# Batches 1 and 2 turned through HBM in an FFT convolution with routed experts

## The chip, the cores and the metric

The kernel runs on one core of one Trainium2 chip. The metric is the device time of one execution in microseconds, the median of the runs. Below, TensorE is PE in the rows, VectorE is DVE, ScalarE is ACT, GpSimd is POOL and SyncE is SP; SyncE issues most DMAs, in order, and GpSimd issues the indirect and the accumulating ones.

## The reference

A convolution over the sequence by FFT, then a mixture of 8 experts with a capacity of 768 tokens each:

```python
X = np.fft.rfft(x, axis=1)                       # x: 8 x 3072 x 256
Y = X * (filt_r + 1j * filt_i)[None]
y = np.fft.irfft(Y, n=3072, axis=1)              # rows of the experts: 24576 x 256
logits = x @ w_gate                              # x is now y, flattened
expert_idx = np.argmax(logits, axis=1)           # first 768 tokens of each expert are kept
h = np.maximum(np.einsum('ecd,edf->ecf', disp, w1), 0.0)
y = np.einsum('ecf,efd->ecd', h, w2)
out[i] = gate_w[i] * y[expert_idx[i], pos[i]]    # zero where not kept
```

## The kernel before

Capacity fills up within the first three of eight batches, so only these are convolved; a guarded branch does all eight if that isn't so. For each batch the FFT is split as 3072 = 96 x 32 (N1 = 96, N2 = 32).

**Forward, first stage** (`a`, L257, matmul in L267). The batch's x comes in eight chunks c of four columns t, each 96 partitions x 4 x 256 fp32 (`load_x`, 384 KB). For each t and each half h of the 256 channels, one fp32 matmul has the x piece (96 x 128) as stationary operand and 128 columns of the constant A as moving operand. The result has the channels on the partitions and is copied by ScalarE into ZA[h] (L271).

**Turn** (`t`, L282, transposes in L290). Six steps k transpose ZA in pieces of 64 x 64 on TensorE; ScalarE copies the two banks of a step to Q (L295), which has (frequency part, t) on its 128 partitions, 24 groups p and 256 channels. For batch 0 some copies are VectorE's.

**Middle stage** (`middle`, L354), six groups g with two halves each. `bm` (L303) multiplies Q with the second-stage constants, VectorE makes the products with the filter (L319), GpSimd adds the pairs (L323, L324), `g` (L336) turns them back, ScalarE and VectorE split that into yh and yl (L339, L340), `bi` (L350) runs the inverse second stage, and ScalarE copies the result to V (L352). Between the halves of the groups stand fill steps, a list of lists: one entry after each half from g = 1 on. They hold the routing of the batch before, zero fills of the output (`zero`, 2 MB each), x loads, and in the last middle stage the first expert's weights.

**Inverse, first stage** (`ai`, L396, matmul in L405). VectorE transposes V in four parts (`ti`, L394); 11 steps for half 0 and 8 for half 1 multiply by AI, ScalarE copies to rt (five buffers) and SyncE stores to ybuf (L411).

**Order around the change.** All is written out by hand, engine by engine in program order. For batch b + 1: four chunks of the first stage, inverse half 0 of batch b, the other four chunks interleaved with the routing's counts (`counts`), the small counting matmuls (L493, L494), six turn steps interleaved with `slots`, then inverse half 1 of batch b with the routing's one-hot masks and table matmuls (L548), and the middle stage of b + 1. The last two inverse steps and the rest of the table run in that middle stage (`ahead`, `fill`).

**Weights of expert 0.** `load_part` gives one load of 1 MB to raw (`load_a`, L694) and four cut steps; a cut copies a quarter to wah and its negative to wal on ScalarE (L699, L703), and after every second cut GpSimd issues a DMA that adds the raw weights to wal (L707). `early_row` gathers rows of ybuf on GpSimd (L568). In the last middle stage the four cuts stand in fill entries 0 to 3.

A tile pool named side holds A, the x chunks and ZA, and is closed ahead of the last middle stage; the expert weights take its place.

Of the kernel before, what the change touches and what calls it, by code (L numbers as in the profile page):

```python
# [9 lines left out]
F32 = mybir.dt.float32  # L10
# [78 lines left out]
def fftconv_moe_kernel(ctx, tc, x, x0, fr, fi, fny, wg, w1, w2, ca, cai, cb, co, out, cap):  # L89
# [23 lines left out]
    yall = dram.tile([NB, N1, N2, CH], F32, name="yall")  # L113
    yrows = ybuf.rearrange("b a t c -> (b a t) c")

    def bank():
        return psum.tile([128, 512], F32, name="ps", tag="ps")
# [45 lines left out]
    def run(fs):  # L163
        for f in fs:
            f()

    class Conv:
# [83 lines left out]
        def load_x(self, b, c):  # L251
            t = self.side.tile([N1, 4, D], F32, name="xt", tag="xt")
            src = x[b] if isinstance(b, int) else x[bass.ds(b, 1)].rearrange("o c a t d -> (o c) a t d")
            nc.sync.dma_start(out=t, in_=src[c])
            self.xts[c] = t
# [13 lines left out]
        def a_out(self, ps, c, h):  # L269
            w = 128 if self.resident else QP  # L270
            nc.scalar.copy(self.ZA[h][:, :, c * 4:c * 4 + 4], ps[:, :4 * w].rearrange("p (t q) -> p q t", q=w)[:, :QP, :])  # L271

# [527 lines left out]
    with tc.manual_schedule():  # L800
# [46 lines left out]
        def rows_in(b, cs, more):  # L847
            steps = []
            for c in cs:
                steps += [lambda c=c: cv.a(c, 0), lambda c=c: cv.a(c, 1)]  # L850
                if more:
                    steps.append(lambda c=c: cv.load_x(b, c + 4))
            return steps

        for b in range(NB0 - 1):
            for c in range(4):
                cv.load_x(b + 1, c)
            cv.middle(V, with_zeros(fill, (3, 6)), ahead)
# [5 lines left out]
            run(rows_in(b + 1, range(4), True))  # L864
            run(halves[0])
            interleave(rows_in(b + 1, range(4, 8), False), counts)
            sums()
            interleave([lambda k=k: cv.t(k) for k in range(NP // 4)], slots)
            if b + 2 == NB0:
# [5 lines left out]
                load_a()  # L875
            S = halves[1]
            run([masks[0], masks[1], S[0], S[1], table[0], masks[2], S[2], S[3], table[1], masks[3], S[4], S[5]])
            ahead = S[6:]
            fill = [[table[2]], table[3:]]

# [22 lines left out]
        fill[0].append(cut_a[0])  # L903
        fill[1] += [early_index, cut_a[1]]
        fill += [[cut_a[2], lambda: early_row(0, 0)], [cut_a[3], load_b, lambda: early_row(0, 1)], [lambda: early_row(0, 2)], [last_fill],
# [198 lines left out]
```

## Time and profile before

| | us |
|---|---|
| median of 3 runs | 491.63 |
| lowest, highest | 491.21, 492.63 |
| profiled execution, whole | 493.73 |
| its span | 492.0 |
| TensorE busy | 478.8 |
| ScalarE busy | 270.4 |
| VectorE busy | 243.3 |
| GpSimd busy | 199.4 |

The first 192 us are the three batches, the rest the experts. A row of the timeline has its start from the span's begin, its length, the engine, the line, the operation, tiles and shapes; xN joins N instructions, and brackets give the idle time ahead of it and what ended that. An fp32 matmul is shown as two instructions (two passes). The chain of waits is followed back from the last instruction.

### The profile page before, as it was taken

The page shows a single profiled execution, that of the slowest core. Times are in us where ns is not written, and L with a number is a line of the kernel's source. Part 1 is how long each engine was busy: PE and PEld are TensorE (multiplying, and loading weights), DVE is VectorE, ACT ScalarE, POOL GpSimd, SP SyncE. Part 2 cuts the span into 40 slices and gives each one's busy share as a digit, 9 for nine tenths or more (in the row PEclk, how much of TensorE's full clock was granted, in tenths as well). Part 3 has the DMA queues.
Part 4 walks back from the last instruction along what each step waited for, and adds up shares of the span by engine and source line. Part 5 has one row for each costly group of instructions (what it writes and reads, how often), then busy time and mean ns, then how long its engine had stood idle before and what let it go on. Part 6 is the DMA issues. An engine that isn't in the chain of part 4 may idle for free.

```text
span 492.0 us, 10406 instructions
## 1 busy us (share of the span) xinstructions
PE 478.8 (97%) x4078; PEld 470.9 (96%) x4078; DVE 243.3 (49%) x549; ACT 270.4 (55%) x626; POOL 199.4 (41%) x243
## 2 busy tenths in 40 slices
PE   8999999999999999999999999999999999999994
PEld 8999999999999999999999999999999999899994
DVE  3587755777737878956432343333423423423510
ACT  3555767456657687665362683383482572573411
POOL 3064120444010885518532754454463462563022
PEclk9999999999999999999999999999999999999999
DMA  8997180890645559377458699979979989984001
GB/s 302 340 329 273 33 225 19 213 381 8 162 112 165 113 150 191 90 216 124 115 158 244 143 228 268 365 200 271 367 209 269 362 208 268 351 158 115 0 24 48
DMA packets 60186, 96.16 MB, mean 195 GB/s; under 512 B 4224, under 2 KB 36704, under 8 KB 60000
## 3 DMA queue, kind: packets, MB, share of 16 engines
q1 hardware_dynamic: 43472, 63.55, 40.0%
q0 software_dynamic: 15344, 29.76, 27.9%
q10 hardware_dynamic: 1312, 2.10, 1.3%
q8 instruction: 34, 0.56, 0.5%
q14 instruction: 24, 0.20, 0.1%
HBM read 55.02 MB, written 40.37 MB: 194 GB/s over the span
## 4 chain that ended last, share of the span: by engine, by line
PE 50%; issue 17%; DMA 14%; POOL 10%; DVE 3%; ACT 3%; POOLq 1%; SPq 0%; ACTq 0%; DVEq 0%
DMA y<-ob,idxs 13%; PE ps L608 10%; PE ps L267 8%; PE ps L660 7%; PE ps L405 6%; PE ps L303 5%; PE ps L336 5%; PE ps L350 4%; POOL rows L568 4%; POOL y L666 2%; POOL wal L707 2%; PE ps L429 2%; POOL wbl L707 1%; PE ps L290 1%; DMA V<-x 1%
## 5 line engine op out<-in xcount | busy, mean ns | idle before, releaser
L660 PE MATMUL ps<-wbh,h 128*128 128x256 f32 x768 | 140.8, 283 | 0.0
L591 DVE SCALAR_TENSOR_TENSOR h<-ps,h 128x384 fp32r<-128x384 f32 x128 | 66.7, 552 | 109.8 <-ACT h L589 94.8
L660 PEld LDWEIGHTS ps<-wbh,h 128*128 128x128 f32 x768 | 119.9, 190 | 0.8 <-issue 0.4
L660 PE MATMUL ps<-wbl,h 128*128 128x256 f32 x384 | 108.3, 282 | 0.7 <-issue 0.7
L666 POOL DMA_INDIRECT y<-ob,idxs x48 | 48.6, 1012 | 115.5 <-ACT ob L663 109.0
L608 PE MATMUL ps<-xh,wah 128*128 128x384 f32 x256 | 86.6, 338 | 1.9 <-ACT ob L663 1.8
L608 PE MATMUL ps<-xl,wah 128*128 128x384 f32 x256 | 86.2, 337 | 0.4 <-DVE xl L593 0.4
L608 PE MATMUL ps<-xh,wal 128*128 128x384 f32 x256 | 86.0, 336 | 0.0
L589 ACT ACTIVATE h<-ps 128x384 fp32r<-128x384 f32 x128 | 58.8, 497 | 37.2 <-PE ps L608 29.4
L660 PEld LDWEIGHTS ps<-wbl,h 128*128 128x128 f32 x384 | 72.9, 190 | 0.9 <-issue 0.9
L663 ACT ACTIVATE ob<-ps,gt 128x256 f32<-128x256 f32 x48 | 22.4, 474 | 80.2 <-PE ps L660 38.8
L323 POOL TENSOR_TENSOR t<-t,t 128x256 f32<-128x256 f32 x33 | 24.9, 755 | 68.4 <-DVE t L319 64.0
L608 PEld LDWEIGHTS ps<-xh,wah 128*128 128x128 f32 x256 | 48.1, 188 | 3.1 <-ACT ob L663 2.9
L568 POOL DMA_INDIRECT rows<-ybuf,idxg x42 | 42.8, 1019 | 16.3 <-issue 11.6
L608 PEld LDWEIGHTS ps<-xl,wah 128*128 128x128 f32 x256 | 48.1, 188 | 0.9 <-DVE xl L593 0.9
L608 PEld LDWEIGHTS ps<-xh,wal 128*128 128x128 f32 x256 | 48.1, 188 | 0.0
L336 PE MATMUL ps<-IG,t 128*128 128x136 f32 x288 | 38.2, 281 | 0.8 <-POOL t L324 0.8
L339 ACT CAST yh<-ps 128x408 fp32r<-128x408 f32 x48 | 23.9, 503 | 27.5 <-PE ps L336 26.0
L593 DVE TENSOR_TENSOR xl<-ps,xh 128x384 fp32r<-128x384 f32 x32 | 16.3, 547 | 44.0 <-ACT xh L589 36.1
L336 PEld LDWEIGHTS ps<-IG,t 128*128 128x128 f32 x288 | 35.4, 190 | 1.5 <-POOL t L324 1.4
L303 PE MATMUL ps<-Bc,Q 128*128 128x128 f32 x288 | 35.8, 276 | 0.0
L303 PEld LDWEIGHTS ps<-Bc,Q 128*128 128x128 f32 x288 | 33.8, 192 | 0.1
(135 smaller groups left out, 772.6 us busy)
## 6 DMA issues: line engine op xcount, KB each, us to landing
y<-zt SPq DMA_DIRECT2D x12, 2048.0 KB, 20.5
raw<-w SPq DMA_DIRECT2D x13, 1024.0 KB, 6.2
wbl<-w POOLq DMA_DIRECT2D x16, 512.0 KB
wal<-w POOLq DMA_DIRECT2D x14, 512.0 KB
xt<-x SPq DMA_DIRECT2D x16, 384.0 KB, 5.9
ybuf<-rt SPq DMA_DIRECT2D x20, 162.0 KB, 2.5
ybuf<-rt SPq DMA_DIRECT2D x16, 192.0 KB, 2.9
Q<-x SPq DMA_DIRECT2D x4, 528.0 KB, 8.3
```

The lines of the kernel that those rows point to most:

```text
L267: nc.tensor.matmul(ps[:, i * w:(i + 1) * w], xt[:, i, h * 128:(h + 1) * 128], A[:, i * QP:i * QP + w], start=True, stop=True)
L303: nc.tensor.matmul(ps[:, i * 128:(i + 1) * 128], self.Q[:, p, h * 128:(h + 1) * 128], self.Bc[:, 1 if p == NP - 1 else 0, :], start=True, ...
L323: eng.tensor_tensor(out=t1[:, :, 0, :], in0=t1[:, :, 0, :], in1=t2[:, :, 1, :], op=ALU.subtract)
L336: nc.tensor.matmul(ps[:, i * 136:(i + 1) * 136], self.ysb[(p // 4, h)][:, (p % 4) * 128:(p % 4 + 1) * 128], self.IG[:, h, :], start=True, ...
L339: nc.scalar.copy(fh[:, o], ps[:, :408])
L405: nc.tensor.matmul(ps[:N1, i * w:(i + 1) * w], AI[:, n0 + i, :], V[h][:, :, n0 + i, :], start=True, stop=True)
L568: nc.gpsimd.indirect_dma_start(out=rows[:, t, :], out_offset=None, in_=yrows[:lim, :], in_offset=bass.IndirectOffsetOnAxis(ap=idx[:, j + t ...
L589: nc.scalar.activation(out=hi, in_=ps, func=AF.Relu if relu else AF.Copy)
L591: nc.vector.scalar_tensor_tensor(out=lo, in0=ps, scalar=0.0, in1=hi.bitcast(F32), op0=ALU.max, op1=ALU.subtract)
L608: nc.tensor.matmul(ps[:, :n * 128], w[:, kk, m * 128:(m + 1) * 128], y[:, kk, o], start=k == 0, stop=k == 5)
L660: nc.tensor.matmul(ps[:, :D], y[:, m, o], w[:, m, :], start=m == 0 and j == 0, stop=m == NF - 1 and j == 2)
L666: ins = nc.gpsimd.indirect_dma_start(out=out, out_offset=bass.IndirectOffsetOnAxis(ap=(idxs if ix is None else ix)[:, j:j + 1], axis=0), i ...
```

## The change

Batch 0 stays. For batches 1 and 2 the first stage has the constants A as stationary operand and a whole x row of 256 channels as moving operand (`a_rows`), so that frequencies lie on the partitions. ScalarE copies two banks of a chunk to a slot of ZA[0] (three slots), and SyncE stores it to a new HBM tensor zturn, 96 rows of 4 KB. When all eight chunks are stored, six loads of 512 KB in pieces of 1 KB (`load_Q`) bring it to Q in the order that the transposes made before. Chunks 4 to 6 of x lie in slots of ZA[1].

The x loads of the next batch move into the fill entries 0 to 3 (in batch 2 behind the last three loads of Q), the zero fills from entries 3 and 6 to 5 and 7. The first block of chunks is three, not four; the counts are interleaved with three chunks and the slots with two. The first weight load of expert 0 moves from ahead of inverse half 1 into fill entry 0 of the last middle stage, its four cuts from entries 0 to 3 into 2 and 3, two each.

```diff
         def load_x(self, b, c):
-            t = self.side.tile([N1, 4, D], F32, name="xt", tag="xt")
+            if self.resident and 4 <= c < NCH - 1:
+                t = self.slot(1, c - 4).rearrange("p (t d) -> p t d", d=D)
+            else:
+                t = self.side.tile([N1, 4, D], F32, name="xt", tag="xt")
...
+        def slot(self, h, k):
+            return self.ZA[h].rearrange("p q t -> p (q t)")[:N1, k * 4 * D:(k + 1) * 4 * D]
+
+        def a_rows(self, c):
+
+            xt, A, z = self.xts.pop(c), self.Ac[c], self.slot(0, c % 3)
+            for k in range(2):
+                ps = bank()
+                for i in range(2):
+                    t = 2 * k + i
+                    nc.tensor.matmul(ps[:QP, i * D:(i + 1) * D], A[:, t * QP:(t + 1) * QP], xt[:, t, :], start=True, stop=True)
+                nc.scalar.copy(z[:, k * 2 * D:(k + 1) * 2 * D], ps[:QP, :])
+            nc.sync.dma_start(out=zturn[:, c * 4:c * 4 + 4, :], in_=z.rearrange("p (t d) -> p t d", d=D))
+
+        def load_Q(self, k):
+
+            src = zturn[k * 16:k * 16 + 16].rearrange("(p j) t c -> (j t) p c", p=4)
+            nc.sync.dma_start(out=self.Q[:, k * 4:k * 4 + 4, :], in_=src)
...
-        def rows_in(b, cs, more):
+        def rows_in(b, cs):
             steps = []
             for c in cs:
-                steps += [lambda c=c: cv.a(c, 0), lambda c=c: cv.a(c, 1)]
-                if more:
-                    steps.append(lambda c=c: cv.load_x(b, c + 4))
+                steps.append(lambda c=c: cv.a_rows(c))
+                if c == 0:
+                    steps.append(lambda: cv.load_x(b, NCH - 1))
             return steps
 
+        loads = []
         for b in range(NB0 - 1):
-            for c in range(4):
-                cv.load_x(b + 1, c)
-            cv.middle(V, with_zeros(fill, (3, 6)), ahead)
+            loads += [lambda b=b, c=c: cv.load_x(b + 1, c) for c in range(NCH - 1)]
+            fill = with_zeros(fill, (5, 7))
+            for i, f in enumerate(loads):
+                fill[i // 2].append(f)
+            cv.middle(V, fill, ahead)
...
-            run(rows_in(b + 1, range(4), True))
+            run(rows_in(b + 1, range(3)))
             run(halves[0])
-            interleave(rows_in(b + 1, range(4, 8), False), counts)
+            interleave(rows_in(b + 1, range(3, 6)), counts)
             sums()
-            interleave([lambda k=k: cv.t(k) for k in range(NP // 4)], slots)
+            interleave(rows_in(b + 1, range(6, 8)), slots)
...
-                load_a()
-            S = halves[1]
-            run([masks[0], masks[1], S[0], S[1], table[0], masks[2], S[2], S[3], table[1], masks[3], S[4], S[5]])
+            S, Q = halves[1], [lambda k=k: cv.load_Q(k) for k in range(NG)]
+            run([Q[0], masks[0], masks[1], S[0], S[1], table[0], masks[2], S[2], Q[1], S[3], table[1], masks[3], S[4], Q[2], S[5]])
             ahead = S[6:]
             fill = [[table[2]], table[3:]]
+            loads = Q[3:]
...
-        fill[0].append(cut_a[0])
-        fill[1] += [early_index, cut_a[1]]
-        fill += [[cut_a[2], lambda: early_row(0, 0)], [cut_a[3], load_b, lambda: early_row(0, 1)], [lambda: early_row(0, 2)], [last_fill],
+        fill[0] += [loads[0], load_a]
+        fill[1] += [early_index] + loads[1:]
+        fill += [[cut_a[0], cut_a[1], lambda: early_row(0, 0)], [cut_a[2], cut_a[3], load_b, lambda: early_row(0, 1)],
+                 [lambda: early_row(0, 2)], [last_fill],
                  [cut_b[0]], [cut_b[1]], [cut_b[2]], [cut_b[3], lambda: early_gate(0)]]
```

The lines of the changed kernel are up to 27 later: L287 is the matmul of `a_rows`, L289 its store, L294 the load of Q, L326 and L359 the matmuls that were L303 and L336, L434 the inverse store that was L411, L717, L722 and L730 the weight load, cut and accumulating DMA that were L694, L699 and L707.

SyncE's program before, from the last x loads of batch 2 through its inverse stores into the last middle stage (AI and constants are loaded long before; both is a small constant):

```order
L254 DMA xt<-x 96x1024 x4
L411 DMA ybuf<-rt 96x3x144 x10
L411 DMA ybuf<-rt 96x2x144
L694 DMA raw<-w 128x2x1024
L411 DMA ybuf<-rt 96x4x128 x6
L762 DMA both<-co 128x144
L411 DMA ybuf<-rt 96x4x128 x2
L694 DMA raw<-w 128x8x256
```

SyncE's program with the change, the same place:

```order
L289 DMA zturn<-ZA_97 96x1024 x5
L294 DMA Q<-zturn 128x4x256
L434 DMA ybuf<-rt 96x4x128 x3
L294 DMA Q<-zturn 128x4x256
L434 DMA ybuf<-rt 96x4x128 x2
L294 DMA Q<-zturn 128x4x256
L434 DMA ybuf<-rt 96x4x128
L785 DMA both<-co 128x144
L434 DMA ybuf<-rt 96x4x128 x2
L294 DMA Q<-zturn 128x4x256
L717 DMA raw<-w 128x2x1024
L294 DMA Q<-zturn 128x4x256 x2
```

The first load of Q stands behind the last five stores and ahead of the inverse stores of half 1, and the weight load raw has moved from ahead of these stores to behind them and four loads of Q.

GpSimd's program before, in the last middle stage, from the pairs of group 1 to the second gather (the t tiles are the products; the two instructions of a pair carry one number):

```order
L323 TENSOR_TENSOR t_2212<-t_2212,t_2213 128x8x32
L324 TENSOR_TENSOR t_2212<-t_2212,t_2213 128x8x32
L707 DMA wal<-w 128x1024
L323 TENSOR_TENSOR t_2259<-t_2259,t_2260 128x8x32
L324 TENSOR_TENSOR t_2259<-t_2259,t_2260 128x8x32
L568 DMA rows_2147<-ybuf,idx_72 128x272
L323 TENSOR_TENSOR t_2275<-t_2275,t_2276 128x8x32
L324 TENSOR_TENSOR t_2275<-t_2275,t_2276 128x8x32
L707 DMA wal<-w 128x1024
L568 DMA rows_2147<-ybuf,idx_72 128x272
```

GpSimd's program with the change, the same place:

```order
L346 TENSOR_TENSOR t_1927<-t_1927,t_1928 128x8x32
L347 TENSOR_TENSOR t_1927<-t_1927,t_1928 128x8x32
L346 TENSOR_TENSOR t_1973<-t_1973,t_1974 128x8x32
L347 TENSOR_TENSOR t_1973<-t_1973,t_1974 128x8x32
L730 DMA wal<-w 128x1024
L591 DMA rows_1861<-ybuf,idx_73 128x272
L346 TENSOR_TENSOR t_1992<-t_1992,t_1993 128x8x32
L347 TENSOR_TENSOR t_1992<-t_1992,t_1993 128x8x32
L730 DMA wal<-w 128x1024
L591 DMA rows_1861<-ybuf,idx_73 128x272
```

The first accumulating DMA has moved from ahead of the first pair of group 2 to behind it, next to the gather and ahead of the second pair.

## Rows read from the trace of the kernel before

**Rows 1.** The page: busy time by engine, and DMA share in 40 slices.
```profile
PE 478.8 (97%) x4078; PEld 470.9 (96%) x4078; DVE 243.3 (49%) x549; ACT 270.4 (55%) x626; POOL 199.4 (41%) x243
...
PE   8999999999999999999999999999999999999994
...
DMA  8997180890645559377458699979979989984001
```

**Rows 2.** Chain of waits: start us, us, what; around the first stage of batch 1.
```profile
57.16 7.14 PE ps L267 x64
64.30 7.89 PE ps L405 x64
72.19 7.16 PE ps L267 x64
...
90.12 1.79 PE ps L303 x16
```

**Rows 3.** Timeline of TensorE, batch 1: turn, inverse half 1, middle stage.
```profile
79.53 3.43 PE L290 MATMUL ps<-ident,ZA 64*128 64x64 f32 x81
...
83.83 2.00 PE L405 MATMUL ps<-V,AI 128*96 128x128 f32 x16
...
89.96 1.95 PE L303 MATMUL ps<-Bc,Q 128*128 128x128 f32 x16
```

**Rows 4.** Timeline: first block of the first stage, and VectorE's transposes of V.
```profile
56.99 7.31 PE L267 MATMUL ps<-A,xt 96*128 96x128 f32 x64
...
57.51 5.04 DVE L394 STREAM_TRANSPOSE V<-V 128x2304 f32<-128x2304 f32 x2 [1.47 <-ACT V L352]
```

**Rows 5.** Landing: inverse stores L411, x loads L254, then two kinds of load.
```profile
DMA to landing us min/median/max: 2.3/2.7/6.2
...
DMA to landing us min/median/max: 4.5/5.9/14.7
...
V<-x SPq DMA_DIRECT2D x1, 272.0 KB, 3.3
...
raw<-w SPq DMA_DIRECT2D x13, 1024.0 KB, 6.2
```

**Rows 6.** Stretches with 1 MB load, then inverse stores alone; last columns DMA share, GB/s.
```profile
150.00:152.00 2.00, 2.00 (x27) 1.93 (x23) 1.71 (x5) 2.00 (x6) 0.00 (x0) 1.00 0.29 39
152.00:154.00 2.00, 2.00 (x25) 1.98 (x24) 1.23 (x3) 2.00 (x6) 0.00 (x0) 1.00 0.86 309
154.00:156.00 2.00, 2.00 (x26) 1.99 (x25) 1.16 (x3) 1.24 (x3) 0.00 (x0) 1.00 1.03 329
...
88.00:90.00 2.00, 2.00 (x25) 2.00 (x22) 1.23 (x3) 1.16 (x2) 0.00 (x0) 1.00 1.00 254
```

**Rows 7.** Timeline of the last middle stage: GpSimd, and TensorE's wait for it.
```profile
165.64 1.11 POOL L707 DMA_DIRECT2D wal<-w  x1 [0.42 <-ACT wal L703]
...
167.65 0.73 POOL L323 TENSOR_TENSOR t<-t,t 128x256 f32<-128x256 f32 x1 [0.90 <-DVE t L319]
...
169.25 1.11 POOL L568 DMA_INDIRECT rows<-ybuf,idx  x1 [0.17 <-issue]
...
171.07 0.72 POOL L324 TENSOR_TENSOR t<-t,t 128x256 f32<-128x256 f32 x1
171.74 0.96 POOL L707 DMA_DIRECT2D wal<-w  x1
...
171.85 0.50 PE L336 MATMUL ps<-IG,t 128*128 128x136 f32 x2 [0.45 <-POOL t L324]
```

**Rows 8.** Timeline of the last middle stage: SyncE's stores and ScalarE.
```profile
160.39 1.63 SPq L411 DMA_DIRECT2D ybuf<-rt  x2
...
161.11 0.58 ACT L407 COPY rt<-ps 96x512 f32<-96x512 f32 x1 [0.99 <-PE ps L405]
...
163.77 0.50 ACT L339 CAST yh<-ps 128x408 fp32r<-128x408 f32 x1 [0.20 <-PE ps L336]
164.16 0.62 ACT L699 CAST wah<-raw 128x512 fp32r<-128x512 f32 x1
...
165.22 0.61 ACT L699 CAST wah<-raw 128x512 fp32r<-128x512 f32 x1
```

More of the change, by code (lines that the diff above doesn't have):

```diff
@@ L113, in fftconv_moe_kernel @@
     yall = dram.tile([NB, N1, N2, CH], F32, name="yall")
+    zturn = dram.tile([4 * NP, N2, D], F32, name="zturn")
     yrows = ybuf.rearrange("b a t c -> (b a t) c")
```

## The prediction

> **What bounds the kernel now.** I read the page's engine line first, then the chain of waits, then the timeline stage by stage, and for the transfers the landing times and the stretches in which they ran. TensorE is busy 97% of the span [rows 1], and in the stretch that the change touches the chain runs on TensorE almost alone [rows 2]: for batch 1, 7.14 us of first-stage matmuls, 7.89 us of inverse matmuls, 7.16 us of first-stage matmuls, then the turn. So what counts is TensorE time taken away, against any wait put into TensorE's queue; SyncE and ScalarE matter only through such waits. Batch 2 repeats the same rows. Everything is summed as a difference in the profiled execution (span 492.0 us, 493.73 us with what lies around it) and then put on the median, 491.63 us; the two differ by more than this kernel's 0.3%, so only the difference carries over. About 0.3%, 1.5 us, is also what a measurement can tell from no change.
>
> **What is removed.** The 48 transposes of a batch run from 79.53, behind the two counting matmuls, to the first matmul of the second inverse half at 83.83 [rows 3]: 4.30 us of TensorE, gone for each of two batches. Their twelve ScalarE copies go too, but ScalarE isn't on the chain apart from the wait inside these 4.30 us.
>
> **First stage turned round.** Before, 64 fp32 matmuls of 128 moving columns; now 32 of 256. Each is two passes, so 7.14 us for 64 passes is 111.6 ns a pass [rows 2]. No 256-column fp32 pass is in the trace. The inverse matmul of 144 columns takes 7.89/64 = 123.3 ns. Continuing the line through both gives 204 ns for 256 columns, doubling the 128-column pass 223 ns. I take 219 ns, proportional to the 144-column row, the nearest in width. 64 passes are then 14.0 us instead of 14.3: 0.3 us saved, with 0 to 1.2 as bounds.
> The first block is now three chunks, 24 passes or 5.26 us from 56.99, and TensorE reaches the first inverse half at 62.25. That half needs VectorE's two transposes of V, done at 57.51 + 5.04 = 62.55 [rows 4]; before, the half began at 64.3 [rows 2] and waited for nothing. This is a new wait of some 0.35 us. **Gain of a batch before the round trip: 4.30 + 0.3 - 0.35 = 4.25 us.**
>
> **Wait for the round trip.** Let T be the end of a batch's last first-stage matmul. From there to the first L303 matmul TensorE has six inverse steps and two table steps left, which took 89.96 - 83.83 = 6.13 us [rows 3]. The first load of Q must have landed by T + 6.13. Its chain: the last copy ends and its store issues at about T + 0.85 (a copy of 96x512 takes 0.58 us [rows 8], and I add 0.27 for its start and SyncE's, an estimate). The store has 384 KB. Stores of 162 and 192 KB land in 2.3 us at the least, with a median of 2.7 [rows 5]; the further 197 KB at 254 to 329 GB/s [rows 6] add 0.6 to 0.8 us: 3.0 us. SyncE then issues the load of 512 KB. Loads of 272 KB land in 3.3 us, of 1 MB in a median of 6.2 [rows 5]. The 1 MB load issued at 150.53 had moved 78 + 618 KB by 154 and its rest by 155.1, so it landed about 4.8 us after issue [rows 6]. From 272 KB upwards 512 KB take 4.05 us, from 1 MB downwards 3.2; I take 3.7. Sum: T + 0.85 + 3.0 + 0.1 + 3.7 = T + 7.65, so **TensorE waits 1.5 us**. With 2.3 and 3.3 it is 0.4 us. With the median 2.7 + 0.8 for the store and, for the load, the x loads' least 4.5 us for 384 KB [rows 5] + 0.4 for the other 128, it is 3.2.
> Rows show 2.3 us for 192 KB, 3.3 for 272 KB and 4.8 to 6.2 for 1 MB. The Trainium skill ("DMA: Bandwidth & Descriptors", Anatomy of one DMA) has a fixed 2.0 us plus the bytes at 436 GB/s, fitted on the other queue kind; by it, as an estimate, store and load take 2.9 and 3.2 us, the wait is 0.9 and the time 1.2 us lower than forecast. It agrees with the small store (2.45) and is too low for the loads (2.6 and 4.4), so I stay with the rows.
> The second load of Q stands in SyncE's queue behind three inverse stores of 192 KB, and they and it run behind the first load. The first load issues at T + 3.95 and its data flow from about T + 5.2 (the 1 MB load had moved 78 KB by 1.5 us after its issue [rows 6]) to 6.8, then 590 KB at 254 GB/s to 9.1, 512 KB to 10.7, landed at T + 11.1. TensorE wants it after the two L303 steps of group 0 (1.79 us [rows 2]) and one inverse step (8 passes, 0.89), at T + 7.65 + 1.79 + 0.89 = T + 10.3: **0.8 us more** (0 if the queue overlaps, 2 if slower). The third load lands by about T + 14 and is wanted after T + 16. **Net gain of a batch: 4.25 - 1.5 - 0.8 = 1.95 us, of two 3.9.**
>
> **Third middle stage.** The weight load raw is moved from ahead of batch 2's second inverse half into the last middle stage, behind the fourth load of Q. In the old clock SyncE is through with the inverse stores at 160.39 + 1.63 = 162.0 [rows 8], so raw issues at about 162.4. At 4.8 us alone plus 1.6 us for the 512 KB ahead it lands at about 168.6. ScalarE reaches the first cut at 164.3 [rows 8] and, being in order, stands for 4.3 us. Two cuts are four instructions at 0.53 us [rows 8], to 170.7. GpSimd's program now has the accumulating DMA wal and the gather between the two product pairs of group 2; the wal waits for these cuts and the second pair is behind it. So: wal 1.11, gather 1.1 with its 0.17, pair 1.4 us, ending at about 174.6, where before it ended at 171.07 + 0.72 = 171.79 [rows 7]. TensorE's L336 waited for just that pair (0.45 us at 171.85), so the shift of 2.8 us lands on TensorE. The second wal waits for ScalarE again (two yh, six V copies, four cuts: 175.2), 0.6 us more, in part absorbed: **3.3 us lost**. If raw were there in time, the moved wal alone would still cost GpSimd 1.1 us, since before it filled a gap (idle 0.90 us right behind it). Each us that raw is later costs one more. Bounds 1.1 to 5.5.
>
> **At nothing.** The stores and x loads of 57 to 80 take the place of four x loads in slices whose DMA share is 1, 8 and 0 tenths [rows 1]. The two zero fills of a batch move behind the x loads and end before the next stores: 2 MB at 329 GB/s [rows 6] is 6.4 us, and entry 7 lies about 10 us ahead of the stage's end. ScalarE's copies go from 12 + 16 to 16. The inverse stores behind SyncE's wait for the round trip are delayed by some 3 us, and five rt buffers hold them for that long; if that cover fails, a TensorE bank wait of a few tenths follows.
>
> **Sum:** -3.9 + 3.3 = -0.6 us, 491.0.
>
> **Rivals.** (a) Both round trips hide: lower bounds everywhere, 2 x (4.25 - 0.4) = 7.7 gained and 1.1 to 2 lost, 485.3 to 486. For it speaks that the DMA engines are idle around 80 us [rows 1]; against it the 1 MB row. (b) The weights come still later: one mechanism, GpSimd standing at wal in the third middle stage behind raw. From 2.1 us later than 168.6 the change is slower than the 0.3%; at 3 us later it is 6.3 - 3.9 = +2.4, 494.0. The x loads' median of 5.9 us for only 384 KB [rows 5] speaks for it, the 329 GB/s against. (c) The round trip at its upper end, waits of 3.2 and then 1.5 us: 2 x (4.25 - 4.7) is 0.9 us lost, with the 3.3 us 495.8; it decides from a wait of 2.6 us a batch in place of 1.5. (d) The front gets shorter and the expert stages give it back, being bound by DMA (9 tenths in most slices from the 24th to the 35th [rows 1]): 491.6. TensorE shows 9 tenths in the same slices, so little speaks for it.
>
> **How the numbers follow.** Forecast 0.42 (488.5 to 493), (a) 0.27, (b) 0.16, (c) 0.10, (d) 0.05. Faster: all of (a) and 0.14 of the forecast, 0.41. Slower: (b) but for 0.02, (c) and 0.04 of the forecast, 0.28. Within 0.3%: 0.31. The range 486.0 to 496.0 leaves out about half of (a)'s low end and of (c). The forecast's own range is 488.5 to 493.
>
> **What would show it.** Per batch, the time from the first L287 matmul to the first L326 matmul should fall from 33.0 to about 30.2 us, with about 1.5 us of TensorE idle before that L326, released by a DMA on Q, and about 0.8 before the next group. 256-column passes at 219 ns. In the third middle stage ScalarE idle for about 4 us before L722, released by a DMA on raw, then GpSimd waiting for it at L730, and L359 for GpSimd. From the end of that stage to the end of the program nothing should change. The forecast is wrong if Q's landing is off by over 1 us, or if raw lands before ScalarE reaches it.

## The result, and the profile after

The changed kernel takes 498.09 us (median of 6 runs, 494.61 to 499.99) against 491.94 us (6 runs, 491.21 to 492.73) for the kernel before: a ratio of 1.0102, 95% interval 1.0074 to 1.0131 (the medians alone are 1.0125 apart). It is slower by 1%, where no change was forecast, and the time lies above the range. The profiled run is one of the quicker ones: 495.47 us, span 493.7, so 1.7 us over the profiled run of before in either measure. A second profiled run of the same kernel, on another chip, is nearer to the median: 498.36 us, span 496.6. Both are used below.

The page of the changed kernel, to be laid beside [rows 1]; the second line is TensorE's granted clock in 40 slices of 12.3 us.

```profile
PE 474.1 (96%) x3758; PEld 459.7 (93%) x3758; DVE 243.6 (49%) x549; ACT 262.3 (53%) x602; POOL 199.7 (40%) x243
...
PEclk9999999999998979999999999999999999999999
DMA  8999186999778786384738699989989989985001
```

TensorE has 320 instructions and 4.7 us less to do, and the span is longer all the same. The two empty slices that the DMA row had (0, from 74 and from 111 us) are now 6 and 9 tenths. The clock row drops from 148 to 160 and from 173 to 185 us (8 and 7); that is around and in the last middle stage.

The chain of waits around the first stage of batch 1 answers to [rows 2] and [rows 3] (start us, us, what).

```profile
56.99 5.16 DVE V L417 x2
...
62.39 8.09 PE ps L428 x64
70.48 5.18 PE ps L287 x24
...
79.55 0.59 ACT ZA L288
...
80.16 2.86 DMA zturn<-ZA
...
83.14 4.41 DMA Q<-zturn
...
87.68 2.02 PE ps L326 x16
```

Where the chain before ran on TensorE alone, it now leaves it for 8.1 us: last copy, last row store (2.86 us to landing), first load of Q (4.41 us), first product of the spectrum. 24 passes of 256 columns took 5.18 us, 216 ns each.

Six landmarks, the starts of instructions in the timelines (us), tell where the gain was made and lost:

| | before | after | after, second profile |
|---|---|---|---|
| batch 1: first first-stage matmul | 57.0 | 56.5 | 56.8 |
| batch 1: first spectrum matmul (L303 before, L326 after) | 90.0 | 87.7 | 87.8 |
| batch 2: first first-stage matmul | 123.5 | 122.3 | 123.3 |
| batch 2: first spectrum matmul | 156.4 | 153.3 | 153.9 |
| first expert's first matmul (L608, L631) | 192.3 | 196.5 | 198.5 |
| end of the span | 492.0 | 493.7 | 496.6 |

Each front, from the first to the second landmark of a batch, is 1.8 to 2.3 us shorter (batch 1: 33.0 to 31.2 or 31.0 us), the middle stage of batch 1 is 1.1 to 2.0 us longer, and 2.5 to 3.1 us are in hand at 156 us. Then the last middle stage takes 43.2 or 44.6 us in place of 35.9. The expert stages give 1.6 to 2.5 us back.

The last middle stage as a stretch of its own, first before, then after, then the second profile of after (stretch, length, then busy us of TensorE, its loads, VectorE, ScalarE, GpSimd; last three: granted clock, DMA share, GB/s):

```profile
156.40:192.30 35.90, 35.06 (x311) 34.20 (x309) 28.74 (x63) 26.49 (x83) 24.40 (x30) 1.00 0.67 151
```
```profile
153.30:196.50 43.20, 39.37 (x308) 38.38 (x309) 28.75 (x63) 26.48 (x83) 24.50 (x30) 0.88 0.79 213
```
```profile
153.90:198.50 44.60, 38.62 (x309) 37.57 (x309) 28.56 (x63) 26.15 (x83) 24.43 (x30) 0.92 0.79 210
```

The instructions are the same (a trace can lack a few records of matmuls), and VectorE, ScalarE and GpSimd are as busy as before. TensorE idles 3.83 us where it idled 0.84, and its matmuls take 4.3 us longer, because the granted clock fell (in the second profile 5.98 and 3.6). In windows of 4 us of the changed kernel (same columns):

```profile
152.00:156.00 4.00, 2.72 (x17) 2.75 (x18) 1.29 (x2) 0.58 (x1) 0.10 (x1) 0.79 1.01 260
156.00:160.00 4.00, 4.00 (x35) 3.96 (x34) 2.51 (x4) 0.89 (x2) 2.72 (x4) 0.78 1.10 336
...
168.00:172.00 4.00, 1.04 (x9) 0.85 (x8) 0.85 (x2) 3.45 (x10) 0.94 (x1) 0.93 0.53 170
172.00:176.00 4.00, 3.36 (x14) 3.04 (x15) 2.97 (x6) 3.11 (x10) 3.59 (x5) 0.50 0.78 122
176.00:180.00 4.00, 4.00 (x26) 4.00 (x26) 1.39 (x3) 2.71 (x10) 3.58 (x5) 0.72 0.98 290
```

A mean of 0.50 over four microseconds is the lower level, 1.2 GHz, throughout. Both stretches at a lowered clock come after a wait of TensorE, 2.03 and 2.96 us, which the timeline shows, with what it waits for (start us, us, engine, line, operation; in brackets the idle time before it and its releaser):

```profile
153.28 2.78 PE L326 MATMUL ps<-Bc,Q 128*128 128x128 f32 x16 [2.03 <-DMA Q<-zturn]
...
161.19 0.55 SPq L717 DMA_DIRECT2D raw<-w  x1
...
168.55 0.62 ACT L722 CAST wah<-raw 128x512 fp32r<-128x512 f32 x1 [5.69 <-DMA Q<-zturn]
...
171.06 1.11 POOL L730 DMA_DIRECT2D wal<-w  x1 [3.34 <-ACT wal L726]
171.15 1.07 DVE L363 TENSOR_TENSOR yl<-ps,yh 128x408 fp32r<-128x408 f32 x2 [3.80 <-ACT yh L362]
...
171.79 2.63 PE L359 MATMUL ps<-IG,t 128*128 128x136 f32 x10 [2.96 <-DVE yl L363]
...
175.06 0.82 PE L359 MATMUL ps<-IG,t 128*128 128x136 f32 x2 [0.64 <-POOL t L347]
```

ScalarE stands for 5.69 us at the first cut of the raw weights. (The releaser printed there is a load of Q; raw itself, issued at 161.19, lands 7.3 us later, at 168.5, and in the second profile the line names raw.) The cut of yh is queued behind it on ScalarE, VectorE's yl waits for yh, and TensorE for yl.

### The profile page after: what moved, and what is told of

It reads as the page before. It is cut to its first block, busy times and chain, and to the rows that moved or that the text cites. A ratio compares the mean times of both kernels' runs of the same rounds, so it can differ in the third digit from the quotient of the medians.

```text
span 493.7 us, 9813 instructions
## 1 busy us (share of the span) xinstructions
PE 474.1 (96%) x3758; PEld 459.7 (93%) x3758; DVE 243.6 (49%) x549; ACT 262.3 (53%) x602; POOL 199.7 (40%) x243
## 4 chain that ended last, share of the span: by engine, by line
PE 73%; issue 10%; DMA 5%; POOL 4%; DVE 4%; ACT 3%; POOLq 0%; SPq 0%; ACTq 0%
PE ps L631 23%; PE ps L683 21%; PE ps L326 6%; PE ps L359 5%; PE ps L428 4%; PE ps L373 4%; PE ps L287 4%; PE ps L271 3%; DVE V L417 2%; POOL y L689 2%; DMA Q<-zturn 2%; PE ps L452 2%; ACT V L375 1%; DMA raw<-w 1%; DMA zturn<-ZA 1%
## 5 line engine op out<-in xcount | busy, mean ns | idle before, releaser
L631 PE MATMUL ps<-xh,wah 128*128 128x384 f32 x256 | 86.5, 338 | 0.6 <-ACT ob L686 0.6
L631 PE MATMUL ps<-xl,wah 128*128 128x384 f32 x256 | 86.2, 337 | 0.4 <-DVE xl L616 0.4
L631 PE MATMUL ps<-xh,wal 128*128 128x384 f32 x256 | 86.0, 336 | 0.0
L631 PEld LDWEIGHTS ps<-xh,wah 128*128 128x128 f32 x256 | 48.1, 188 | 1.4 <-ACT ob L686 1.2
L631 PEld LDWEIGHTS ps<-xl,wah 128*128 128x128 f32 x256 | 48.1, 188 | 0.9 <-DVE xl L616 0.9
L631 PEld LDWEIGHTS ps<-xh,wal 128*128 128x128 f32 x256 | 48.1, 188 | 0.0
L359 PE MATMUL ps<-IG,t 128*128 128x136 f32 x288 | 39.8, 289 | 3.8 <-DVE yl L363 3.0
L326 PE MATMUL ps<-Bc,Q 128*128 128x128 f32 x288 | 36.9, 281 | 5.0 <-DMA Q<-zturn 4.2
L359 PEld LDWEIGHTS ps<-IG,t 128*128 128x128 f32 x288 | 36.9, 197 | 4.6 <-DVE yl L363 3.1
L326 PEld LDWEIGHTS ps<-Bc,Q 128*128 128x128 f32 x288 | 34.6, 195 | 5.7 <-issue 4.6
L616 DVE TENSOR_TENSOR xl<-ps,xh 128x384 fp32r<-128x384 f32 x32 | 16.2, 547 | 45.5 <-ACT xh L612 45.5
```

The source lines that it names most:

```text
L326: nc.tensor.matmul(ps[:, i * 128:(i + 1) * 128], self.Q[:, p, h * 128:(h + 1) * 128], self.Bc[:, 1 if p == NP - 1 else 0, :], start=True, ...
L359: nc.tensor.matmul(ps[:, i * 136:(i + 1) * 136], self.ysb[(p // 4, h)][:, (p % 4) * 128:(p % 4 + 1) * 128], self.IG[:, h, :], start=True, ...
L631: nc.tensor.matmul(ps[:, :n * 128], w[:, kk, m * 128:(m + 1) * 128], y[:, kk, o], start=k == 0, stop=k == 5)
```

## The experiments

The runs stand in four groups, each on a chip of its own with the kernel before beside it; before was 496.36, 492.20, 493.88 and 495.18 us there, so ratios are compared, and times only within a group. The changed kernel ran beside its variants in the second group alone; across groups only ratios stand side by side. Its own two profiles differ by 1.4 us in the last middle stage (43.2 and 44.6), so a smaller difference in one profile of a variant says little. Of the first two theories, one is that the last middle stage is lost to raw's late landing and ScalarE's place in the queue, the rival that the round trip of Q itself, or the clock behind its wait, is what costs.

**Raw weights loaded earlier.**

```
-            run([Q[0], masks[0], masks[1], S[0], S[1], table[0], masks[2], S[2], Q[1], S[3], table[1], masks[3], S[4], Q[2], S[5]])
+            early_load = [load_a] if b + 2 == NB0 else []
+            run([Q[0], masks[0], masks[1], S[0], S[1], table[0], masks[2], S[2], Q[1]] + early_load
+                + [S[3], table[1], masks[3], S[4], Q[2], S[5]])
...
-        fill[0] += [loads[0], load_a]
+        fill[0] += [loads[0]]
```


> The changed kernel with one move: expert 0's first weight load (raw, 1 MB) is issued behind the second load of Q, ahead of three inverse stores, and no longer behind the fourth load of Q; the cuts stay in fill entries 2 and 3. Theory 1 (in the last middle stage ScalarE stands at the first cut for raw, GpSimd at wal, TensorE for 3.0 us at L359, and TensorE's clock is low after that): the 5.7 us of ScalarE idle and the 3.0 us of TensorE idle go, the stretch from 168 to 180 us is at full clock, and the time falls by 4 to 6 us, to 492 to 494. Rival (the round trip of Q is the whole loss, and the last middle stage only follows): within 1 us of the changed kernel's 498.

499.17 us, ratio 1.0051 (1.0015 to 1.0088). ScalarE reaches the first cut at 163.75 and waits for nothing there, yet the last middle stage is 42.7 us. TensorE's waits in 145 to 200 us, then one of ScalarE's (line waited for: us, times, longest):

```profile
PE ps L326 <- DMA Q<-zturn: 3.8, 2, 2.3
PE ps L359 <- POOL t L347: 3.2, 4, 1.7
```
```profile
ACT wbh L722 <- DMA raw<-w: 3.4, 1, 3.4
```

The wait has moved: to the loads of Q behind raw, to GpSimd's pairs, and to the raw load of w2. By the ratios about half of the loss is gone, not all; 4 to 6 us had been expected.

**TensorE kept at work while Q is awaited**, with eight matmuls on zeros ahead of the middle stages of batches 1 and 2.

```
+            ps = bank()
+            warm(8)
```


> The changed kernel with eight idle matmuls of 128 columns (16 passes, 1.8 us) on TensorE between the last inverse step and the first L326 of batches 1 and 2, that is inside the wait for Q of 2.0 to 2.2 us; nothing reads them. Theory 1 (TensorE's clock falls because TensorE stood still, and that costs beside the wait itself): no clock of 0.79 between 152 and 160 us in batch 2, the L326 there at 1.8 us for 16 and not 2.8, 1.5 to 2.5 us less in all; the low clock behind the 3 us wait at L359 may stay. Rival (the clock falls for another reason, as the whole power of the chip): clock and time as without, within 1 us.

502.96 us, ratio 1.0135 (1.0056 to 1.0214). Windows and waits of this kernel:

```profile
150.00:160.00 10.00, 9.48 (x93) 9.08 (x91) 5.36 (x12) 3.47 (x7) 0.65 (x1) 1.00 0.78 227
...
170.00:180.00 10.00, 5.31 (x30) 4.80 (x29) 4.07 (x8) 6.59 (x18) 5.12 (x6) 0.77 0.67 166
```
```profile
PE ps L359 <- DVE yl L363: 4.0, 1, 4.0
```
```profile
ACT wah L722 <- DMA raw<-w: 6.8, 1, 6.8
```

The clock stays at 1.00 across the wait for Q. That TensorE's idling is what takes it down is not shown by this, for in the second profile of the changed kernel it stayed at 1.00 behind that wait as well (1.72 us, windows of 152 to 160 us). And the time that a full clock saves at the stage's start is waited for later: yl 4.0 us instead of 3.0. Raw is issued 7.3 us behind the first spectrum matmul where it was 7.9, but then takes 8.5 us to the first cut instead of 7.4; why it takes longer is open. The stage is 43.7 us long.

**Batch 1 alone, twice.** The first stage, the stores and the loads as changed for batch 1; batch 2 and the last middle stage as before, but for the fill entries of the x loads and zero fills.

```
-            run(rows_in(b + 1, range(3)))
...
+            if b == 0:
+                run(rows_in(b + 1, range(3)))
...
+            else:
+                run(rows_old(b + 1, range(4), True))
+                run(halves[0])
+                interleave(rows_old(b + 1, range(4, 8), False), counts)
+                sums()
+                interleave([lambda k=k: cv.t(k) for k in range(NP // 4)], slots)
```


> The change for batch 1 alone; batch 2 and the last middle stage as in the kernel before, but for the x loads, which stay in fill entries. Theory 1 (batch 1 gains 4.3 and pays 2.2 for Q's landing, 0.8 behind ScalarE's rt copy and 0.6 for V, its clock stays up): the kernel before less 0.7 us, 490.5 to 491.8, and its runs lie as close together as those of before. Rival (the added 12 MB of DMA traffic slow the rest down, or the clock falls in batch 1 too): 493 or more.

> The change for batch 1 alone, in the order of the changed kernel, once more on a chip with the next one. 0.994 to 1.001 of before: 4.3 us of TensorE removed, 2.3 us of waiting for the first load of Q added, about 0.6 for V and 0.7 for the PSUM of the inverse.

Ratios 0.9974 (0.9941 to 1.0006) and 0.9995 (0.9978 to 1.0012): no change that can be measured. What the change takes off TensorE in a batch it gives back within the batch: in the two profiles the front of batch 1 is 1.6 and 1.2 us shorter than before and its middle stage 1.7 and 1.8 us longer, with a clock of 0.50 to 0.67 behind the wait for Q. The loss belongs to batch 2, behind which the weights are loaded.

**No round trip.** Q is loaded from x, so that no load waits for a row store, and the convolution of batches 1 and 2 is left out of the result.

```
...
-            src = zturn[k * 16:k * 16 + 16].rearrange("(p j) t c -> (j t) p c", p=4)
+            src = x[b].rearrange("c a t d -> (c a t) d")[k * 512:(k + 1) * 512].rearrange("(p j) d -> j p d", p=4)
```


> The changed kernel with Q loaded from x itself, in the same pieces of 1 KB, so that the loads wait for no store; the stores to zturn stay, but nothing reads them, and the convolution of batches 1 and 2 is left out in that sense. Theory 1: the first load of Q is issued 2.8 us earlier and is there before TensorE wants it, so the 2.2 and 2.0 us at L326 go and the clock holds through batch 2's start; the last middle stage still loses some 3 us at L359 and the clock behind it. 4 us for the waits and 2 for the clock: 491 to 493. Rival (the last middle stage is the whole loss): 497 or more.

497.69 us, ratio 1.0003 (0.9972 to 1.0034), level with before. Beside the 1.0110 that the changed kernel has on another chip, the wait for the stores is worth about 1%, some 5 us, as much as the whole loss; how much of that is TensorE's waits and how much its clock, the run doesn't tell. But the round trip had its place in the prediction's sum (1.5 and 0.8 us in each of two batches). The other part of the loss stays: the last middle stage still takes 43.0 us, with ScalarE waiting 5.0 us for raw.

```profile
ACT wah L722 <- DMA raw<-w: 5.0, 1, 5.0
```

**The changed kernel again, and without raw.** In the second kernel the raw load of w1 is left out and w1 is cut from a constant in SBUF; the first expert's hidden layer is then computed from other numbers.

```
...
-                (load_a, cut_a), (load_b, cut_b) = (load_part(0, part, raw0, w0, 4) for part in "ab")
+                load_a, cut_a = load_part(0, "a", raw0, w0, 4, other=cv.F[0].rearrange("p n f -> p (n f)"))
+                load_b, cut_b = load_part(0, "b", raw0, w0, 4)
...
-        fill[0] += [loads[0], load_a]
+        fill[0] += [loads[0]]
```


> The changed kernel itself, on one chip with the kernels beside it. Both theories: 1.007 to 1.013 of before (3.5 to 6.5 us longer), first product of the spectrum to first product of the first expert about 43 us in the last middle stage (35.9 before).

> The changed kernel without the load of the first expert's raw weights w1 (1 MB on SyncE's queue); they are cut from a constant in SBUF instead, so the first expert's hidden layer is computed from other numbers; all instructions on the compute engines stay. Theory 1 (raw, late behind four loads of Q, is what the last middle stage ends on): that stage falls from 43 to 37 or 38 us, and the time by 5 us against the changed kernel. Theory 2 (the loads of Q and the stores of the inverse alone hold the stage): it stays at 41 us or more.

498.08 us, 1.0110 (1.0094 to 1.0127), against 494.38 us, 1.0052 (1.0029 to 1.0075), on one chip: raw is worth 3.7 of the 5.9 us by the medians, 2.9 of 5.4 by the ratios. The last middle stage without it, and TensorE's waits there:

```profile
153.20:192.80 39.60, 35.33 (x309) 34.28 (x309) 28.74 (x63) 26.33 (x83) 24.32 (x30) 1.00 0.82 208
```
```profile
PE ps L326 <- DMA Q<-zturn: 4.0, 2, 2.2
PE ps L359 <- POOL t L347: 2.0, 3, 1.6
```

39.6 us instead of 44.6, at full clock. It missed the 37 or 38 us expected: the second group's wait for Q (2.2 us) and GpSimd's pairs keep TensorE idle for 4.3 us.

**Half of Q.** Each load of Q for batch 2 brings 256 KB instead of 512.

```
-            nc.sync.dma_start(out=self.Q[:, k * 4:k * 4 + 4, :], in_=src)
+            n = 2 if half else 4
...
+            nc.sync.dma_start(out=self.Q[:, k * 4:k * 4 + n, :], in_=src)
```


> The changed kernel, where each load of Q for batch 2 brings two of its four pairs of frequencies (256 KB instead of 512 KB) and the others keep what batch 1 left there: the convolution of batch 2 comes out of half its data; all instructions on the compute engines stay. Theory 1 (in the last middle stage the bytes of Q, of the inverse's stores and of the raw weights share the DMA engines): the wait on Q at the second group goes, raw lands 2 us or more sooner after the first stage's end, that stage falls from 43 to 39 us or less and the time by 3 to 4 us against the changed kernel. Theory 2 (what counts is the number of transfers in turn on the queue, each with its latency, whatever the bytes): no more than 1 us.

496.65 us, 1.0068 (1.0044 to 1.0092), and a stage of 42.0 us. Both theories miss a part. The first load lands in 3.06 us instead of 4.28 (batch 2 of the first profile), the wait for it falls to 0.86 us, and the second group no longer waits for Q. Raw lands 2 us sooner (first cut at 166.47), but 1.7 of them are its earlier issue (159.49) and only 0.4 a shorter transfer. And ScalarE still waits 5.3 us for it, having itself come earlier.

**What sets raw's landing, and what ends the stage.** The landmarks of the last middle stage (us) in all kernels in which ScalarE stood at the first cut for over a microsecond:

| kernel | first spectrum | last copy to rt | raw issued | first cut | first expert | from cut to expert |
|---|---|---|---|---|---|---|
| after | 153.28 | 159.70 | 161.19 | 168.55 | 196.51 | 28.0 |
| after, second profile | 153.93 | 161.55 | 163.04 | 170.10 | 198.46 | 28.4 |
| filled wait | 156.73 | 162.57 | 164.06 | 172.52 | 200.42 | 27.9 |
| no round trip | 151.18 | 157.03 | 158.52 | 165.23 | 194.20 | 29.0 |
| half of Q | 152.34 | 158.00 | 159.49 | 166.47 | 194.35 | 27.9 |

Raw is issued 1.49 us behind the start of ScalarE's last copy to rt in every row: SyncE has the last inverse store and one load of Q ahead of it, and that store waits for the copy. The copy waits for TensorE's last inverse step, which runs in this stage. The chain of waits of the changed kernel has just this way:

```profile
156.06 1.71 PE ps L428 x8
157.76 0.98 PE ps L326 x8
158.74 0.89 PE ps L428 x8
...
159.70 0.59 ACT rt L430
...
160.30 0.30 SPq L434
...
160.66 0.47 SPq L294
```

Before, that copy came 4.7 us behind the first spectrum matmul (161.11 [rows 8] and 156.44). In the changed kernel it came 6.4 us behind, as TensorE ran at 0.79 and 0.78; in the second profile 7.6, after 2.10 us of waiting for Q's second load and then at 0.57; in the other three 5.7 to 5.9, with a wait of 0.7 or 0.9 us and at full clock.

The stage ends 28 to 29 us behind raw's landing in these kernels, whatever TensorE did up to then. Before, the first cut, which waited for nothing, was 30.7 us ahead of the first expert:

```profile
161.59 0.62 ACT L699 CAST wah<-raw 128x512 fp32r<-128x512 f32 x1
```

It is 30.7 too with raw loaded earlier (163.75 to 194.47), and 29.3 without raw (163.47 to 192.77). So with about 28 us from the cut on, these have 1 to 3 us to spare there, and something else ends their stage.

**Cuts two entries later**, so that ScalarE doesn't stand at the first one.

```
-        fill += [[cut_a[0], cut_a[1], lambda: early_row(0, 0)], [cut_a[2], cut_a[3], load_b, lambda: early_row(0, 1)],
-                 [lambda: early_row(0, 2)], [last_fill],
-                 [cut_b[0]], [cut_b[1]], [cut_b[2]], [cut_b[3], lambda: early_gate(0)]]
+        fill += [[lambda: early_row(0, 0)], [lambda: early_row(0, 1)], [cut_a[0], cut_a[1], lambda: early_row(0, 2)],
+                 [cut_a[2], cut_a[3], load_b, last_fill], [], [], [cut_b[0], cut_b[1]], [cut_b[2]], [cut_b[3], lambda: early_gate(0)]]
```


> The changed kernel with the cuts of the first expert's w1 and the load of its w2 two entries of the last middle stage later (entries 4 and 5 where they stood in 2 and 3; the cuts of w2 in entries 8 to 10 where they stood in 6 to 9); the raw load of w1 is issued where it was, and the same bytes move. Theory 1 (head of line: ScalarE stands 5 us at the first cut because raw has not landed, and with it the splits and the pairs queued behind it on ScalarE and GpSimd, so TensorE idles and its clock falls): ScalarE's wait on raw goes, TensorE's wait for yl in 165 to 176 us goes, the stage falls from 43 to 39 or 40 us, as without the raw load, and the time by 3 to 4 us against the changed kernel, to 1.003 to 1.006 of before. Theory 2 (the DMA engines' bytes set the stage, wherever ScalarE waits): the stage stays at 42 us or more, the waits go to Q, to w2's raw or to the end of the stage, and the time stays at 1.009 or more.

502.94 us, 1.0162 (1.0132 to 1.0192): worse. The stand at the first cut is gone (0.74 us) and yl isn't waited for. The wait reappears at the end of the stage (145 to 230 us, TensorE and ScalarE):

```profile
PE ps L359 <- POOL t L347: 5.2, 3, 4.3
```
```profile
ACT wbh L722 <- DMA raw<-w: 7.9, 2, 4.6
```

The raw load of w2 uses the same buffer and can't start before w1 is cut: it is issued at 179.79 where it was issued at 174.67, and GpSimd's accumulating load for w2 holds back the last pairs. So I no longer take it for the place of one cut in ScalarE's queue, but for the whole row of raw, cuts, raw, cuts through one buffer; this is read from the trace.

**More work between the last store and the first use of Q.** All eight chunks stand ahead of the inverse's first half; its second half and the routing follow. The first kernel has this for batch 1 alone (below); the second has it for batch 2 too, with raw among the stores of the inverse's first half and two of the routing's tables in the last middle stage.

```
+                run(rows_in(b + 1, range(NCH)))
...
+                run(H0[:4] + [Q[0]] + H0[4:8] + [Q[1]] + H0[8:] + [Q[2]])
+                interleave(S[:4], counts)
+                sums()
+                interleave(S[4:], slots)
+                masks[0]()
```


> The change for batch 1 alone, in another order: all eight chunks of the first stage stand ahead of the inverse of the batch before, the loads of Q are issued among that inverse's first stores, and the inverse's second half and the routing follow ahead of the middle stage; batch 2 and the last stage are as before. Theory 1 (order: the trip through HBM costs what TensorE waits for, and here 14 us of inverse steps stand between the last row store and the first use of Q): no wait on Q, so the gain is the 4.3 us of transposes less 0.6 for V: 3.5 us under before. Theory 2 (traffic: the 6 MB of added transfers slow the batch wherever they stand): no more than the 0.7 us that the change of batch 1 in its first order gave.

> As the kernel with batch 1 in the other order, with batch 2 in that order too: the raw weights are loaded among the stores of the inverse's first half, 20 us ahead of their first cut, and two of the routing's four tables move into the last middle stage. Theory 1: twice the gain, 7 us under before, of which the expert stages may give back 2 to 3: 484 to 489 where before is 491 to 492; first to last of the last middle stage 36 to 38 us, with no wait on Q or on raw. Theory 2: the last middle stage stays at 42 us or more, since its traffic is the same, and the time is not under before.

497.94 us, 1.0128 (1.0105 to 1.0151), and 501.44 us, 1.0167 (1.0144 to 1.0190): slower where the first theory had a gain; the second, that the added traffic alone limits the batch, isn't what the traces show either. TensorE no longer waits for Q at all. Batch 1's chain of waits, and two windows, of the first of the two kernels:

```profile
75.23 5.10 DMA ybuf<-rt
...
81.41 0.23 POOL L L433
...
88.82 0.60 DVE ol L562
89.42 0.27 DVE ohh L563
89.70 3.68 DVE t L342 x6
```
```profile
90.00:98.00 8.00, 6.85 (x62) 6.44 (x62) 8.00 (x13) 1.32 (x3) 5.28 (x7) 1.00 0.99 284
98.00:106.00 8.00, 7.27 (x64) 6.80 (x63) 8.00 (x14) 3.54 (x14) 4.92 (x8) 1.00 1.04 229
```

The chain is now VectorE's. The routing, which before ran beside the first stage and the turn, falls together with the middle stage: VectorE is busy 16.0 of 16 us and TensorE 14.1. The routing's largest step (ol) also takes longer there, 1091 ns in the mean against 680 before. The routing's start is late too: a store of the inverse, whose buffer the next copy needs, takes 5.10 us to land beside the loads of Q. The order that hides the load of Q takes away what the routing was hidden behind.

**Smaller transfers** for batch 1 alone: the last row store in two, the first load of Q in two.

```
...
-            nc.sync.dma_start(out=self.Q[:, k * 4:k * 4 + 4, :], in_=src)
+            n = 4 if k else 2
+            for p in range(k * 4, k * 4 + 4, n):
+                src = zturn[p * 4:p * 4 + 4 * n].rearrange("(p j) t c -> (j t) p c", p=n)
+                nc.sync.dma_start(out=self.Q[:, p:p + n, :], in_=src)
```


> The change for batch 1 alone, with the last row store sent as two of 2 KB pieces and the first load of Q as two of 256 KB, so that the first product of the spectrum waits for less. Theory 1 (the wait for Q is the latency of one store and one load, each with a part that goes by its bytes): about 0.4 us less for the store and 0.6 us less for the load, wait on Q from 2.3 to 1.3 us, 1 us under the kernel without the split. Theory 2 (the latency does not go by bytes, or the smaller transfers queue behind each other): no change of the wait.

Ratio 1.0009 (0.9985 to 1.0033) against 0.9995 without the split on the same chip. TensorE's first two groups:

```profile
86.90 2.24 PE L331 MATMUL ps<-Bc,Q 128*128 128x128 f32 x16 [1.27 <-DMA Q<-zturn]
...
91.52 1.13 PE L331 MATMUL ps<-Bc,Q 128*128 128x128 f32 x8 [1.49 <-DMA Q<-zturn]
```

The first wait falls from 2.74 to 1.27 us, as expected, and the second group, whose load stands one place further back, waits 1.49. The sum is the same, and so is the median. (In the profiles the clock fell without the split, to 0.60 and 0.55 in 90 to 94 us, and stayed at 1.00 with it, and batch 1 takes 65.8 us instead of 67.1; the medians don't show it.) None of the kernels beats before by more than can be measured.

## Why the prediction was wrong

- **What is removed** held: the turn and its twelve copies are gone, and a 256-column pass took 216 ns where 219 was taken. The new wait for V was 0.5 us in the mean of two, where 0.35 was taken.
- **The round trip** was somewhat short. The store took 2.86 us (3.0), the load of Q 4.41 (3.7), so TensorE waited 2.2 and 2.0 us instead of 1.5. The 0.8 us at the second group came true in batch 1 in that size (0.80), though released by ScalarE's copy of an inverse step instead of a load. In the second profile batch 2's second group waited for Q itself, 2.1 us. A front should have been 2.8 us shorter and was 1.8 to 2.3; at 156 us 4.7 us should have been in hand (2.75 for each front less 0.8), and 2.5 to 3.1 are. The Trainium skill ("DMA: Bandwidth & Descriptors", Anatomy of one DMA) has 2.0 us plus the bytes at 436 GB/s, fitted on GpSimd's queue: as an estimate 2.9 us for the store, which the trace agrees with, and 3.2 us for the load, which it doesn't.
- **The last middle stage is the step that failed**: 3.3 us were taken (4.1 with the 0.8 of batch 2's second group, which falls in it), 7.3 and 8.7 measured. Who waits for whom was as described, ScalarE standing at the first cut, GpSimd at its accumulating load and L359 behind both. What was mis-sized is raw's landing. That it landed at 168.55, the very 168.6 forecast, is luck: 168.6 is a time in the kernel before, and with 3.9 us gained raw should have landed at 164.7. Counted from batch 2's first spectrum matmul, 168.6 - 156.4 = 12.2 us were taken, 13.0 with that 0.8, and 168.55 - 153.3 = 15.3 measured (second profile 16.2). This is rival (b), weights 3 us later, at 0.16. Its 494.0 is a difference of +2.4 us, and the two profiled runs differ by +1.7; the medians differ by 6.2.
- **Why raw came later.** One part is the issue: 6.8 us behind that matmul by the prediction (162.4 - 156.4 + 0.8), 7.9 measured and 9.1 in the second profile. Subtracting the front's gain from it was sound, as raw's issue does follow TensorE's last inverse step; but the way to that step became longer, in the first profile by TensorE at a lowered clock, for which the sum has no term, in the second by 2.10 us of waiting for Q in place of 0.8. The other part is the transfer, 7.4 us to the first cut (7.1) where 6.2 were taken.
- **From raw's landing to the stage's end** the sum was short as well: 12.2 + 28.0 would have made a stage of 40.2 us, 4.3 over before, not 3.3. Part of this is TensorE at half clock (0.50 in 172 to 176 us), for which the prediction had no term.
- **Together:** by the prediction the first expert begins at 192.3 - 0.6 = 191.7 us, and in the first profile it began at 196.5. Of these 4.8 us, 1.5 are missing in the fronts, 1.1 lie in raw's issue, 1.2 in its transfer and 1.0 between its landing and the stage's end.
- **A batch's gain**, 1.95 us net, was not found: the change for batch 1 alone gave at most 1.1 us in the closer of its two measurements (0.9978 to 1.0012). In both its profiles the clock fell to 0.50 to 0.67 behind the wait for Q, which the sum has no term for.
- **"Nothing changes after that stage"** was wrong in the other direction. In the profiled run 4.2 us are lost at the first expert and 1.7 at the end. Waits of TensorE from 190 us on, of before and of after:

```profile
PE ps L608 <- ACT ob L663: 1.8, 2, 1.0
PE ps L660 <- issue: 0.7, 1, 0.7
```
```profile
PE ps L631 <- ACT ob L686: 0.6, 1, 0.6
```

- **Slips that change nothing.** Raw's landing adds up to 168.8 by its own terms (162.4 + 4.8 + 1.6), not 168.6, and the lower end of rival (a) to 485.0, not 485.3.
- **Left open.** Removing raw explains 3.7 of 5.9 us (same chip, medians). Of the rest, the trace without raw shows waits for Q and GpSimd's pairs; these were not taken away together with raw. That raw's transfer takes 6.7 to 8.5 us to the first cut where 6.2 were taken is read from the traces alone; which of the transfers beside it does that was not told apart. Nor is it shown why the profiled runs of one kernel differ by 2.9 us; 0.6 us come from before the last middle stage, 1.4 from that stage and 0.9 from the experts. Loading both raw parts into buffers of their own was not tried.

## What to carry to other kernels

A transfer that is moved in a queue written by hand is issued when the entry ahead of it is. Find what that entry waits for in the new program, follow this back to the engine that it hangs on, and put that engine's new waits and its clock into the sum, then the bytes that now run beside the transfer. Follow it also to the end of what hangs on it: here moving the wait (earlier load, later use, smaller pieces) gave back half of the loss at best and otherwise only gave the wait another name. And an order that hides one engine's wait can uncover another engine: with all chunks ahead of the inverse, VectorE's routing had nothing left to hide behind.

## What the runs showed of the hardware

TensorE's clock came down to its lower level after waits of about 2 to 4 us, and the same matmuls then cost 2.0 to 4.3 us more in the last middle stage of the changed kernel (either profile) and of five of its variants (raw earlier, filled wait, no round trip, half of Q, later cuts), but only 0.3 us in the one without raw. Length alone doesn't decide it. That kernel waited 2.2 us for Q at full clock, and so did the changed kernel in batch 1 of the first profile (2.16 us), while its wait of 2.03 us in batch 2 was followed by 0.79. With eight matmuls on zeros in the wait the clock stayed at 1.00, as it did in the second profile without them.

The first load of Q for batch 2 took 3.06 us for 256 KB and 4.28 us for 512 KB: 262,144 bytes more in 1.22 us, or 215 GB/s (one load each, in the profiles of two kernels), less than the 329 GB/s [rows 6] by which the prediction stepped from its rows to 512 KB.
